# Key sums side by side, copied by two engines, and a choice whose second half moves: a linear-attention and mixture-of-experts kernel

## The chip, the cores and the metric

The kernel runs on one core of a Trainium2 chip. A core has TensorE (PE, matrix products; its weight loads are shown apart as PEld), VectorE (DVE), ScalarE (ACT), GpSimd (POOL) and SyncE (SP, which here starts DMA transfers). Each engine takes its own instructions in order and waits on semaphores for the others. PSUM is the memory that TensorE writes; it lies in banks of 512 float32 per partition. The metric is device time in microseconds (us).

## The reference

Linear attention over 8 batches, 8 heads, 576 tokens and 64 dimensions, with 128 random features, and then a layer of 8 experts to which each of the 4608 tokens is sent by its largest logit:

```python
q_p, k_p = phi(q_s), phi(k_s)              # exp of projections less their maximum
kv = np.einsum('bhsm,bhsd->bhmd', k_p, v)  # key sums
z = np.sum(k_p, axis=2)
num = np.einsum('bhsm,bhmd->bhsd', q_p, kv)
den = np.einsum('bhsm,bhm->bhs', q_p, z)[..., None] + 1e-06
x = (num / den) as [4608, 512]
logits = xn @ en.T / tau                   # xn, en: rows over their norms
expert_idx = np.argmax(logits, axis=1)
out[mask] = gate_w[mask, None] * (np.maximum(x[mask] @ w1[e], 0.0) @ w2[e])
```

## The kernel before, in words

The tokens are cut into 36 tiles of 128. Two batches share nine tiles, and so a key sum (over one batch) closes after the fourth-and-a-half and the ninth tile of a group: eight closes in all. One loop (L652 to L737) does attention; its iteration i handles keys of tile i and queries of tile i - 6, so iterations 0 to 5 have keys alone, 6 to 35 both, 36 to 41 queries alone (the tail), and 42 the last numerators. After the loop come a table of expert steps, worked out on VectorE while TensorE does filler work, and the expert part, 38 steps of matrix products.

Inside an iteration the order is written out by hand for all five engines. The names that the text uses, with what they do:

- `proj` (L321): projections, k in one PSUM bank and q in another; each iteration does two pairs, "one" and "two". Each pair is four products for two banks.
- `maxima` (L329), on VectorE: the largest of 128 features of four heads, `nmk` for keys and `nmq` for queries. `feats` (L334), on ScalarE: the exponentials.
- `qtr` (L395): transposes of the query features of the tile before into the two banks of `nub`; the prediction calls it the turn. `qcopy` (L403) copies one bank with ScalarE and the other with VectorE into `qp`.
- `num` (L412): query features times key sums, into the same two banks. `num_out` (L422), on VectorE: `rr` (denominator and its inverse), `xr` (the tile's rows), `lg` (their logits).
- `kvmm` (L341): key features times values, added up in two banks, `kv0` for one half of the heads and `kv1` for the other. The values have a column of ones, which gives z.
- `kv_closed` (L358): a finished key sum is copied to `kvs` by ScalarE in two halves, and by GpSimd into another order in `kvc`. In the next iteration `kv_turn` transposes it, `kv_turned` copies that back, `kv_logits` (kve in the prediction) multiplies it with the experts' vectors into the last columns of the second bank of `nub`, and `kv_logits_out` copies these into `kvs`.
- `routed` (L439): the choice for three tiles. Its steps: the logits' sum; their maximum `mx` and `raw`; the selection `sel` (L465 to L467, three steps on VectorE); the prefix, eight small products (L473, L475) into the second bank of `nub`; `base` and `run` (L481, L482) on VectorE, which read it; and then places and stores by GpSimd.
- `first_steps` (L542): expert work that is known early, taken out step by step with `next(fill)` as filler.

Work that is to be done at a place of a later iteration is put into tables by place: `mid`, `after`, `then` and `ends`, in the order in which the iteration comes to them (`mid` behind `qcopy`, `after` behind `num`, `then` ahead of `kvmm`, `ends` at its end). L730 says at which places the steps of a choice stand.

Of the kernel before, what the change touches and what calls it, by code (L numbers as in the profile page):

```python
# [11 lines left out]
F32 = mybir.dt.float32  # L12
# [4 lines left out]
AF = mybir.ActivationFunctionType  # L17
ALU = mybir.AluOpType
# [4 lines left out]
P = 128  # L23
B, H, S, D, M = 8, 8, 576, 64, 128
# [15 lines left out]
NPRE = 2  # L40
PADP = 6
FILLS = 1, 2, 2, 2, 2, 0
FILL1, FILL2, FILL3 = 6, 11, 6
# [12 lines left out]
def attention_moe(ctx: ExitStack, tc: tile.TileContext, qT, kT, v1, omT, emb, tau, w1q, w2q, xs, out):  # L56
# [222 lines left out]
    with ExitStack() as c1:  # L279
# [61 lines left out]
        def kvmm(i, a, b):  # L341
# [7 lines left out]
            for h in range(4):  # L349


                for c in range(0, P, 64):
# [3 lines left out]
                    )  # L356

        def kv_closed(sb, b):  # L358
            kvs[sb, b] = p1.tile([P, H, D + 1 + E], F32, name=f"kvs{sb}_{b}", tag="kvs", bufs=2)
            for a in range(2):  # L360
                nc.scalar.activation(kvs[sb, b][:, 4 * a : 4 * a + 4, 0 : D + 1], kva[sb, b, a], AF.Copy)
            kvc = xgp[NPRE][:, 0:DM].rearrange("p (h d) -> p h d", h=H)
            nc.gpsimd.tensor_copy(
                kvc.rearrange("p (c a) d -> p a c d", a=2), kvs[sb, b][:, :, 0:D].rearrange("p (a c) d -> p a c d", a=2)
            )
            st["kvc", sb, b] = kvc

        def kv_turn(sb, b):
            kvc = st["kvc", sb, b]
            st["kvtr", sb, b] = tr = ps.tile([P, 512], F32, name=f"kvtr{sb}_{b}", tag="kv0")  # L370
            for c in range(4):
                nc.tensor.transpose(tr[:, c * P : (c + 1) * P], kvc[:, 2 * c : 2 * c + 2, :].rearrange("p a d -> p (a d)"), ident)

# [15 lines left out]
        def kv_logits_out(sb, b):  # L389
            nc.vector.tensor_copy(  # L390
                kvs[sb, b][:, :, D + 1 :].rearrange("p (a c) e -> p c a e", a=2),
                st["kve", sb, b].rearrange("p c (a e) -> p c a e", a=2),
            )
# [15 lines left out]

        pn = nub[:, :, 0 : 4 * (D + 1 + E)].rearrange("p a (h w) -> p a h w", h=4)  # L410

        def num(i):  # L412
            sb, u = divmod(i, TPS)
            for a in range(2):
                for h in range(4):
                    for z, b in enumerate((u > 4, u >= 4)):
                        nc.tensor.matmul(
                            pn[z * 64 : z * 64 + 64, a, h, :], st["qp", i, z][:, 4 * a + h, :], kvs[sb, int(b)][:, 4 * a + h, :],
                            start=True, stop=True,
                        )  # L420

        def num_out(i):  # L422
# [3 lines left out]
            if gi == 0:  # L426
                st["lg", g] = small.tile([P, G, H, E], F32, name=f"lg{g}", tag="lg", bufs=2)
            rr = small.tile([P, 2, 4], F32, name=f"rr{i}", tag="rr", bufs=3)
            nc.vector.tensor_scalar(rr, pn[:, :, :, D], EPS, None, op0=ALU.add)
            nc.vector.reciprocal(rr, rr)  # L430
            by = lambda w: rr.unsqueeze(3).to_broadcast([P, 2, 4, w])
            nc.vector.tensor_tensor(
                xr[:, 0:DM].rearrange("p (h a d) -> p a h d", a=2, d=D), pn[:, :, :, 0:D], by(D), op=ALU.mult,
            )
            nc.vector.tensor_tensor(
                st["lg", g][:, gi].rearrange("p (a h) e -> p a h e", a=2), pn[:, :, :, D + 1 :], by(E), op=ALU.mult,
            )
# [200 lines left out]

        mid, after, then, ends = {}, {}, {}, {}
        at = lambda d, *key: d.setdefault(key, [])  # L640
# [4 lines left out]
        def go(d, *key):  # L645
            for f, *a in d.pop(key, ()):
                f(*a)
# [4 lines left out]
        for i in range(END + 1):  # L652
# [22 lines left out]
            elif qs:  # L675
                two = [("q", iq, a, ("px", "py")[i % 2]) for a in range(2)]
            proj(*one)
            if ts:
                qtr(iq - 1)
            for p in one[:1]:  # L680
                maxima(*p)
            proj(*two)
            if ts:
                qcopy(iq - 1, 1, True)
                qcopy(iq - 1, 0, False)
            go(mid, i)
            for p in one[:1]:
                feats(*p)
            if i == END:
                next(fill)  # L690
            for p in one[1:] or two[:1]:
                maxima(*p)
            if ts:
                num(iq - 1)
            go(after, i)
            for p in two[1:]:
                maxima(*p)
# [12 lines left out]
            for x in sums:  # L710
                kvmm(*x)
            closed = ss and u in (4, 8)
            if closed and not qs:
# [13 lines left out]
            if ts and iq % G == 0 and iq < NTILE:  # L727
                steps = routed(iq // G - 1)
                next(steps)
                for d, key in ((ends, i + 1), (mid, i + 2) if i >= NTILE else (ends, i + 1), (after, i + 2), (ends, i + 2), (ends, i + 2), (ends, i + 3), (ends, i + 4)):  # L730
                    at(d, min(key, END)).append((next, steps, None))
# [6 lines left out]
        loop.close()  # L738
        assert not any((mid, after, then, ends)), (mid, after, then, ends)
        steps = routed(NTILE // G - 1)  # L740
# [396 lines left out]
def layout(inputs):  # L1137
# [13 lines left out]
    for u in range(TPS + 1):  # L1151
        rows = slice(0, D) if u == 4 else slice(D, P) if u == 5 else slice(0, P)
        v1[:, u, rows, :, :D] = v[:, u - (u > 4), rows]
        v1[:, u, rows, :, D] = 1
    v1 = v1.reshape(NSB * (TPS + 1), P, H, D + 1)
# [28 lines left out]
```

## Time and profile before

| | |
|---|---|
| median of 3 runs | 657.77 us (657.25 to 657.97) |
| profiled execution | 658.2 us, span 656.4 us |
| PE busy | 631.7 us (96%) |
| DVE busy | 497.3 us (76%) |
| ACT busy | 416.9 us (64%) |
| POOL busy | 328.5 us (50%) |
| granted TensorE clock, mean | 0.996 of full speed |

A row of the profile names the line, the engine, the operation, the tile written and the tiles read, with partitions x elements. In a wait the engine on the left waited for the one on the right. A busy TensorE need not be one at its peak, since matrix products are pipelined and their ends are modelled. Attention with its tail lasts to about 217 us, and the expert part from there to the end.

### The profile page before, as it was taken

The numbers are of one execution on the slowest core, as the hardware profiler recorded it, in microseconds if no ns is written. First come the engines' busy times: TensorE is split into PE (matmuls) and PEld (weight loads), VectorE is DVE, ScalarE is ACT, GpSimd is POOL, SyncE is SP. The second block draws the span as 40 slices with busy tenths as digits, with TensorE's granted clock in tenths as the row PEclk, the third lists the DMA queues.
The fourth block names the chain that finished last, engine by engine and source line by source line (L and its number), as shares of the span: only waits on it lengthen the run. The fifth ranks groups of instructions, "written<-read, shape, count | busy, mean of one in ns | idle before, by whom it ended". The sixth has DMA issues, their size and how long they took to land. (4 is left out here: it accounts for less than half of the span.)

```text
span 656.4 us, 18641 instructions
## 1 busy us (share of the span) xinstructions
PE 631.7 (96%) x6339; PEld 532.1 (81%) x6340; DVE 497.3 (76%) x952; ACT 416.9 (64%) x1074; POOL 328.5 (50%) x414
## 2 busy tenths in 40 slices
PE   8999999998889999999999999999999999999993
PEld 7899999988877787888788888888888888888872
DVE  4789888899888736778787777777768787777771
ACT  6899899899877236645656565656555656565430
POOL 2013443448885425474556364646455554646352
PEclk9999999999999999999999999999999999999998
DMA  7547667678832388588898888978697878887710
GB/s 252 177 148 228 196 202 212 214 243 285 261 125 97 118 308 259 156 237 198 237 211 223 208 227 190 240 193 232 178 244 184 236 192 196 225 208 212 187 64 34
DMA packets 142362, 131.89 MB, mean 201 GB/s; under 512 B 106742, under 2 KB 106870, under 8 KB 142272
## 3 DMA queue, kind: packets, MB, share of 16 engines
q1 hardware_dynamic: 135808, 110.04, 62.8%
q0 software_dynamic: 6320, 20.38, 7.9%
q8 instruction: 57, 0.93, 0.6%
q10 hardware_dynamic: 144, 0.26, 0.2%
q14 instruction: 33, 0.27, 0.1%
HBM read 83.78 MB, written 21.97 MB: 161 GB/s over the span
## 5 line engine op out<-in xcount | busy, mean ns | idle before, releaser
L241 PE MATMUL nu<-w2h,hl 128*128 (+1 forms) x288 | 113.9, 395 | 0.4 <-DVE hl L948 0.4
L241 PE MATMUL nu<-w2h,hh 128*128 (+1 forms) x288 | 113.9, 396 | 0.0
L241 PE MATMUL nu<-w2l,hh 128*128 (+1 forms) x288 | 113.8, 395 | 0.0
L241 PE MATMUL pa<-w1h,xl 128*128 (+1 forms) x280 | 110.8, 396 | 0.4 <-DVE xl L947 0.4
L241 PE MATMUL pa<-w1h,xh 128*128 (+1 forms) x280 | 111.1, 397 | 0.0
L241 PE MATMUL pa<-w1l,xh 128*128 (+1 forms) x280 | 110.6, 395 | 0.0
L909 ACT ACTIVATE pl<-pa 128x512 uint16<-128x512 uint16 x68 | 40.1, 594 | 94.2 <-PE pa L241 56.0
L905 DVE TENSOR_REDUCE wd<-t 128x1024 uint16<-128x1024 uint16 x68 | 90.0, 1325 | 1.7 <-DMA t<-pl 1.7
L338 ACT ACTIVATE ftk<-pjk,nmk 128x128 f32<-128x128 f32 x288 | 84.9, 427 | 6.3 <-DVE nmk L331 6.0
L207 POOL TENSOR_TENSOR w1l<-raww,w1h 128x1024 f32 x34 | 83.7, 2461 | 7.4 <-DVE w1h L206 5.5
L905 DVE TENSOR_REDUCE pl<-pa 128x512 uint16<-128x512 uint16 x68 | 46.6, 688 | 51.6 <-ACT pl L909 51.5
L338 ACT ACTIVATE ftq<-pjq,nmq 128x128 f32<-128x128 f32 x288 | 80.0, 430 | 8.7 <-DVE nmq L331 7.8
L207 POOL TENSOR_TENSOR w2l<-raww,w2h 128x1024 f32 x34 | 82.1, 2415 | 2.4 <-issue 2.4
L327 PE MATMUL pjq<-om,qt 64*128 64x128 f32 x576 | 75.6, 283 | 1.1 <-ACT ftk L338 0.7
L327 PE MATMUL pjk<-om,kt 64*128 64x128 f32 x576 | 76.3, 285 | 0.3 <-DVE om L602 0.3
L944 ACT ACTIVATE hh<-wd 128x1024 fp32r<-128x1024 f32 x34 | 36.1, 1062 | 60.2 <-DVE wd L905 54.3
L327 PEld LDWEIGHTS pjk<-om,kt 64*128 64x128 f32 x576 | 65.1, 190 | 2.9 <-DVE om L602 0.6
L271 POOL DMA_INDIRECT y<-xgp x20 | 22.7, 1136 | 87.6 <-DVE xgp L248 84.1
L241 PEld LDWEIGHTS nu<-w2h,hl 128*128 128x128 f32 x288 | 54.0, 188 | 13.9 <-DVE hl L948 0.8
L327 PEld LDWEIGHTS pjq<-om,qt 64*128 64x128 f32 x576 | 63.9, 188 | 1.6 <-ACT ftk L338 0.9
L241 PEld LDWEIGHTS nu<-w2l,hh 128*128 128x128 f32 x288 | 54.1, 188 | 13.1
L241 PEld LDWEIGHTS nu<-w2h,hh 128*128 128x128 f32 x288 | 54.1, 188 | 13.0
(311 smaller groups left out, 1270.0 us busy)
## 6 DMA issues: line engine op xcount, KB each, us to landing
raww<-w1q SPq DMA_DIRECT2D x38, 512.0 KB, 3.9
raww<-w2q SPq DMA_DIRECT2D x38, 512.0 KB, 5.2
qt<-qT SPq DMA_DIRECT2D x36, 256.0 KB, 4.3
kt<-kT SPq DMA_DIRECT2D x35, 256.0 KB, 3.0
xgp<-xs SPq DMA_DIRECT2D x20, 260.5 KB, 2.8
xg<-xs SPq DMA_DIRECT2D x18, 260.5 KB, 2.9
rf<-w1q SPq DMA_DIRECT2D x4, 512.0 KB, 5.6
rf<-w2q SPq DMA_DIRECT2D x4, 512.0 KB
```

The source lines that it names most:

```text
L207: il = nc.gpsimd.tensor_tensor(at(l, dp), raw, at(h, dp).bitcast(F32), op=ALU.subtract)
L241: done.append(nc.tensor.matmul(dst, x[:, c * P : (c + 1) * P], ws.rearrange("p o f -> p (o f)"), start=(begin and i == 0 and k == 0), stop ...
L271: w = nc.gpsimd.indirect_dma_start(out=out, out_offset=bass.IndirectOffsetOnAxis(ap=xg[:, PAY - 1 : PAY].bitcast(I32), axis=0), in_=xg[:, ...
L327: nc.tensor.matmul(st["pj" + w, i, a][:, c, :], st[w, i][r, c, :], om[r, :], start=True, stop=True)
L338: nc.scalar.activation(ft[:, h, :], pj[:, h, :], AF.Exp, bias=nm[:, h : h + 1])
L905: nc.vector.tensor_reduce(to, src.unsqueeze(2), axis=AX.X, op=ALU.max)
L909: nc.scalar.activation(planes[1][:, o : o + 512], halved(src)[:, :, 1], AF.Copy)
L944: nc.scalar.activation(hh, wd[:, 0:F], AF.Relu)
```

## The change

Four things, in the diff's order.

Key sums: a head of the first half now has its logit columns and the ones ahead of its 64 values, a head of the second half has them behind, so that the values of two heads touch in `kvs`. ScalarE copies one half and VectorE the other. The transposes read `kvs`, and GpSimd's copy goes. The first bank of `nub` gets `num` from column 132 on, the second from column 0, so that one access pattern (`heads`) reaches both.

Query-only iterations (36 to 41): the query projections stand ahead of `qtr`, the first maximum ahead of `qcopy`, the second behind it.

Filler: in iterations 39 to 41 one step is taken between `qcopy` and `num`, and one less at the end.

The choice of the main loop (nine of them, in iterations 11, 14, ... 35): the selection moves from the end of the iteration before to the place `then`, and the prefix from `after` to a new place `late`, behind `kvmm`.

```diff
@@ -39,7 +39,7 @@
 LAG = 6
 NPRE = 2
 PADP = 6
-FILLS = 1, 2, 2, 2, 2, 0
+FILLS = 1, 2, 1, 1, 1, 0
 FILL1, FILL2, FILL3 = 6, 11, 6
 NSTAT = 38
 WARM = 26
@@ -355,21 +355,20 @@
                         start=begin and h == 0, stop=u == 4 + 4 * b and h == 3,
                     )
 
+        HW = D + 1 + E
+
+        def spread(x, *dims):
+            return bass.AP(tensor=x.tensor, offset=x.offset, ap=[x.ap[0], *([a, n] for a, n in dims)])
+
         def kv_closed(sb, b):
-            kvs[sb, b] = p1.tile([P, H, D + 1 + E], F32, name=f"kvs{sb}_{b}", tag="kvs", bufs=2)
-            for a in range(2):
-                nc.scalar.activation(kvs[sb, b][:, 4 * a : 4 * a + 4, 0 : D + 1], kva[sb, b, a], AF.Copy)
-            kvc = xgp[NPRE][:, 0:DM].rearrange("p (h d) -> p h d", h=H)
-            nc.gpsimd.tensor_copy(
-                kvc.rearrange("p (c a) d -> p a c d", a=2), kvs[sb, b][:, :, 0:D].rearrange("p (a c) d -> p a c d", a=2)
-            )
-            st["kvc", sb, b] = kvc
+            kvs[sb, b] = p1.tile([P, 4, 2 * HW], F32, name=f"kvs{sb}_{b}", tag="kvs", bufs=2)
+            nc.scalar.activation(kvs[sb, b][:, :, E : HW], kva[sb, b, 0], AF.Copy)
+            nc.vector.tensor_copy(kvs[sb, b][:, :, HW : HW + D + 1], kva[sb, b, 1])
 
         def kv_turn(sb, b):
-            kvc = st["kvc", sb, b]
             st["kvtr", sb, b] = tr = ps.tile([P, 512], F32, name=f"kvtr{sb}_{b}", tag="kv0")
             for c in range(4):
-                nc.tensor.transpose(tr[:, c * P : (c + 1) * P], kvc[:, 2 * c : 2 * c + 2, :].rearrange("p a d -> p (a d)"), ident)
+                nc.tensor.transpose(tr[:, c * P : (c + 1) * P], kvs[sb, b][:, c, E + 1 : E + 1 + P], ident)
 
         def kv_turned(sb, b):
             kvt = xgp[NPRE][:, 0:DM].rearrange("p (c m) -> p c m", c=4)
@@ -388,7 +387,7 @@
 
         def kv_logits_out(sb, b):
             nc.vector.tensor_copy(
-                kvs[sb, b][:, :, D + 1 :].rearrange("p (a c) e -> p c a e", a=2),
+                spread(kvs[sb, b].rearrange("p c w -> p (c w)"), (2 * HW, 4), (HW + D + 1, 2), (1, E)),
                 st["kve", sb, b].rearrange("p c (a e) -> p c a e", a=2),
             )
 
@@ -407,7 +406,14 @@
                 tc.declare_no_dep(c.ins, st["cp", 1].ins.name, reason="another bank")
 
 
-        pn = nub[:, :, 0 : 4 * (D + 1 + E)].rearrange("p a (h w) -> p a h w", h=4)
+        flat = nub.rearrange("p a x -> p (a x)")
+        o0 = P + E // 2
+        pn = [nub[:, a, o : o + 4 * HW].rearrange("p (h w) -> p h w", h=4) for a, o in ((0, o0), (1, 0))]
+
+        def heads(o, at1, n):
+
+            x = 512 + at1 - o0 - o
+            return flat[:, o0 + o : o0 + o + 2 * x].rearrange("p (a x) -> p a x", a=2)[:, :, 0 : 4 * HW].rearrange("p a (h w) -> p a h w", h=4)[:, :, :, 0:n]
 
         def num(i):
             sb, u = divmod(i, TPS)
@@ -415,7 +421,7 @@
                 for h in range(4):
                     for z, b in enumerate((u > 4, u >= 4)):
                         nc.tensor.matmul(
-                            pn[z * 64 : z * 64 + 64, a, h, :], st["qp", i, z][:, 4 * a + h, :], kvs[sb, int(b)][:, 4 * a + h, :],
+                            pn[a][z * 64 : z * 64 + 64, h, :], st["qp", i, z][:, 4 * a + h, :], kvs[sb, int(b)][:, h, a * HW : (a + 1) * HW],
                             start=True, stop=True,
                         )
 
@@ -426,14 +432,14 @@
             if gi == 0:
                 st["lg", g] = small.tile([P, G, H, E], F32, name=f"lg{g}", tag="lg", bufs=2)
             rr = small.tile([P, 2, 4], F32, name=f"rr{i}", tag="rr", bufs=3)
-            nc.vector.tensor_scalar(rr, pn[:, :, :, D], EPS, None, op0=ALU.add)
+            nc.vector.tensor_scalar(rr.unsqueeze(3), heads(E, D, 1), EPS, None, op0=ALU.add)
             nc.vector.reciprocal(rr, rr)
             by = lambda w: rr.unsqueeze(3).to_broadcast([P, 2, 4, w])
             nc.vector.tensor_tensor(
-                xr[:, 0:DM].rearrange("p (h a d) -> p a h d", a=2, d=D), pn[:, :, :, 0:D], by(D), op=ALU.mult,
+                xr[:, 0:DM].rearrange("p (h a d) -> p a h d", a=2, d=D), heads(E + 1, 0, D), by(D), op=ALU.mult,
             )
             nc.vector.tensor_tensor(
-                st["lg", g][:, gi].rearrange("p (a h) e -> p a h e", a=2), pn[:, :, :, D + 1 :], by(E), op=ALU.mult,
+                st["lg", g][:, gi].rearrange("p (a h) e -> p a h e", a=2), heads(0, D + 1, E), by(E), op=ALU.mult,
             )
 
         def routed(g):
@@ -636,7 +642,7 @@
             nc.vector.tensor_copy(enbd[D:P, :, 1, :], ev[D:P])
 
 
-        mid, after, then, ends = {}, {}, {}, {}
+        mid, after, then, late, ends = {}, {}, {}, {}, {}
         at = lambda d, *key: d.setdefault(key, [])
         for i, f in ((1, emb0), (2, emb1), (4, emb2), (5, emb3)):
             at(ends, i).append((f,))
@@ -674,26 +680,31 @@
                 one = [("k", i, a, ("px", "py")[i % 2]) for a in range(2)]
             elif qs:
                 two = [("q", iq, a, ("px", "py")[i % 2]) for a in range(2)]
-            proj(*one)
+            proj(*(one if ks else two))
             if ts:
                 qtr(iq - 1)
-            for p in one[:1]:
+            for p in (one if ks else two)[:1]:
                 maxima(*p)
-            proj(*two)
+            if ks:
+                proj(*two)
             if ts:
                 qcopy(iq - 1, 1, True)
                 qcopy(iq - 1, 0, False)
+            for p in () if ks else two[1:]:
+                maxima(*p)
             go(mid, i)
+            if NTILE + 2 < i < END:
+                next(fill)
             for p in one[:1]:
                 feats(*p)
             if i == END:
                 next(fill)
-            for p in one[1:] or two[:1]:
+            for p in one[1:]:
                 maxima(*p)
             if ts:
                 num(iq - 1)
             go(after, i)
-            for p in two[1:]:
+            for p in two[1:] if ks else ():
                 maxima(*p)
             u = (i - 1) % TPS
             sums = [(j, a, b) for j, b in ([(i - 2, 1)] if u == 5 else []) + [(i - 1, int(u > 4))] for a in range(2)] if ss else []
@@ -709,6 +720,7 @@
                     maxima(*p)
             for x in sums:
                 kvmm(*x)
+            go(late, i)
             closed = ss and u in (4, 8)
             if closed and not qs:
                 kv_closed((i - 1) // TPS, u // 4 - 1)
@@ -727,7 +739,7 @@
             if ts and iq % G == 0 and iq < NTILE:
                 steps = routed(iq // G - 1)
                 next(steps)
-                for d, key in ((ends, i + 1), (mid, i + 2) if i >= NTILE else (ends, i + 1), (after, i + 2), (ends, i + 2), (ends, i + 2), (ends, i + 3), (ends, i + 4)):
+                for d, key in ((ends, i + 1), (mid if i >= NTILE else then, i + 2), (after if i >= NTILE else late, i + 2), (ends, i + 2), (ends, i + 2), (ends, i + 3), (ends, i + 4)):
                     at(d, min(key, END)).append((next, steps, None))
             go(ends, i)
             if NTILE < i <= END:
...
@@ -1150,8 +1162,10 @@
     v1 = np.zeros((NSB, TPS + 1, P, H, D + 1), v.dtype)
     for u in range(TPS + 1):
         rows = slice(0, D) if u == 4 else slice(D, P) if u == 5 else slice(0, P)
-        v1[:, u, rows, :, :D] = v[:, u - (u > 4), rows]
-        v1[:, u, rows, :, D] = 1
+        v1[:, u, rows, 0::2, 1:] = v[:, u - (u > 4), rows, 0::2]
+        v1[:, u, rows, 0::2, 0] = 1
+        v1[:, u, rows, 1::2, :D] = v[:, u - (u > 4), rows, 1::2]
+        v1[:, u, rows, 1::2, D] = 1
     v1 = v1.reshape(NSB * (TPS + 1), P, H, D + 1)
     w2 = np.asarray(inputs["moe_w2"]).reshape(E, NQ, 2, P, DM).transpose(0, 1, 3, 2, 4)
     return {
```

TensorE around the choice of iteration 11, before. `sel` is the selection, `tri` and `one` are constants, `kva` the key sum of `kvmm`, `pjk` and `pjq` the next iteration's projections; `num` stands above these rows.

```order
L475 LDWEIGHTS one_75
L475 MATMUL nub<-sel_127,one_75 64x16
L475 LDWEIGHTS one_75
L475 MATMUL nub<-sel_127,one_75 64x8
L353 MATMUL kva_0_0_1014<-vt10v,ftk_0_1045 64x65 x8
L353 MATMUL kva_0_1_1023<-vt10v,ftk_1_973 64x65 x8
L327 MATMUL pjk_1_1202<-om,kt_920 128x128
L327 MATMUL pjq_0_1203<-om,qt_924 128x128
```

And in the changed kernel, from the last product of `num` on (`kvs`, `qp`); the rest of the prefix and then the projections follow.

```order
L423 MATMUL nub<-kvs_1_911,qp_1_1101 64x73
L353 MATMUL kva_0_0_1012<-vt10v,ftk_0_1043 64x65 x8
L353 MATMUL kva_0_1_1021<-vt10v,ftk_1_971 64x65 x8
L479 LDWEIGHTS tri
L479 MATMUL nub<-sel_127,tri 64x32
L481 LDWEIGHTS one_75
L481 MATMUL nub<-sel_127,one_75 64x24
L481 LDWEIGHTS one_75
L481 MATMUL nub<-sel_127,one_75 64x16
```

The prefix has moved behind the 16 instructions of `kvmm`.

VectorE at the same place, before: maximum and difference of the logits, the selection, and the first rows of iteration 11 up to `rr`.

```order
L460 TENSOR_TENSOR raw0_916<-raw0_916,mx0_1051 128x24
L465 SCALAR_TENSOR_TENSOR sel0_127<-raw0_916,iotm_83 128x24
L466 TENSOR_REDUCE mx0_1051<-sel0_127 128x3
L467 TENSOR_TENSOR sel0_127<-iotm_83,mx0_1051 128x24
L331 TENSOR_REDUCE nmk11_1_1094<-pjk11_1_1068 128x4
L405 COPY qp4_0_1108<-nub_126 128x512
L331 TENSOR_REDUCE nmq5_0_1115<-pjq5_0_1069 128x4
L331 TENSOR_REDUCE nmq5_1_1141<-pjq5_1_1097 128x4
L331 TENSOR_REDUCE nmk11_0_1148<-pjk11_0_1096 128x4
L429 TENSOR_SCALAR rr4_1168<-nub_126 128x8
```

And in the changed kernel.

```order
L466 TENSOR_TENSOR raw0_914<-raw0_914,mx0_1049 128x24
L331 TENSOR_REDUCE nmk11_1_1089<-pjk11_1_1063 128x4
L404 COPY qp4_0_1103<-nub_126 128x512
L331 TENSOR_REDUCE nmq5_0_1110<-pjq5_0_1064 128x4
L331 TENSOR_REDUCE nmq5_1_1128<-pjq5_1_1092 128x4
L471 SCALAR_TENSOR_TENSOR sel0_127<-raw0_914,iotm_83 128x24
L472 TENSOR_REDUCE mx0_1049<-sel0_127 128x3
L473 TENSOR_TENSOR sel0_127<-iotm_83,mx0_1049 128x24
L331 TENSOR_REDUCE nmk11_0_1138<-pjk11_0_1091 128x4
L435 TENSOR_SCALAR rr4_1166<-nub_126 128x8
```

The three rows of the selection have moved from ahead of four full passes (`nmk`, `qp`, `nmq`, `nmq`) to behind them; `rr` follows one pass later.

VectorE in the tail, iteration 38, before: from a split of early expert work (`w1h`) to the first read of `num`.

```order
L229 TENSOR_TENSOR w1h_106<-fs_x0_4699,w1h_106 128x512
L405 COPY qp31_0_4737<-nub_126 128x512
L465 SCALAR_TENSOR_TENSOR sel1_128<-raw9_4585,iotm_83 128x24
L466 TENSOR_REDUCE mx9_4690<-sel1_128 128x3
L467 TENSOR_TENSOR sel1_128<-iotm_83,mx9_4690 128x24
L331 TENSOR_REDUCE nmq32_0_4742<-pjq32_0_4725 128x4
L331 TENSOR_REDUCE nmq32_1_4768<-pjq32_1_4726 128x4
L429 TENSOR_SCALAR rr31_4772<-nub_126 128x8
```

And in the changed kernel.

```order
L229 TENSOR_TENSOR w1h_106<-fs_x0_4691,w1h_106 128x512
L331 TENSOR_REDUCE nmq32_0_4727<-pjq32_0_4701 128x4
L404 COPY qp31_0_4731<-nub_126 128x512
L331 TENSOR_REDUCE nmq32_1_4733<-pjq32_1_4702 128x4
L471 SCALAR_TENSOR_TENSOR sel1_128<-raw9_4577,iotm_83 128x24
L472 TENSOR_REDUCE mx9_4682<-sel1_128 128x3
L473 TENSOR_TENSOR sel1_128<-iotm_83,mx9_4682 128x24
L435 TENSOR_SCALAR rr31_4764<-nub_126 128x8
```

One maximum now stands ahead of the copy `qp`, the other one and the selection behind it.

## Rows read from the trace of the kernel before

**Rows 1.** Stages of the run: length, busy time by engine, clock, DMA, GB/s.

```profile
41.00:172.00 131.00, 127.14 (x2958) 120.38 (x2956) 117.55 (x298) 120.67 (x424) 62.07 (x169) 1.00 0.70 220
...
217.00:600.00 383.00, 381.88 (x1670) 306.66 (x1669) 285.09 (x457) 214.45 (x398) 200.73 (x110) 1.00 0.82 215
```

**Rows 2.** Waits of TensorE over the run: us in total, times, longest.

```profile
PE nub L417 <- DVE qp L405: 5.1, 8, 1.7
PE nub L400 <- DVE run L482: 1.8, 3, 0.9
...
PE nub L400 <- DVE lg L435: 0.6, 1, 0.6
```

**Rows 3.** Order of time, TensorE, one iteration without a choice: start, length, instruction.

```profile
51.83 0.66 PE L400 MATMUL nub<-ident,ftq 64*128 64x64 f32 x16
...
53.48 1.25 PE L417 MATMUL nub<-kvs,qp 128*64 128x73 f32 x32
...
55.59 0.37 PE L327 MATMUL pjk<-om,kt 64*128 64x128 f32 x1
...
56.58 0.66 PE L400 MATMUL nub<-ident,ftq 64*128 64x64 f32 x16
```

**Rows 4.** Order of time, TensorE and VectorE, one iteration with a choice.

```profile
46.62 0.18 DVE L465 SCALAR_TENSOR_TENSOR sel<-raw,iotm 128x24 bf16<-128x24 f32 x1
...
46.67 0.66 PE L400 MATMUL nub<-ident,ftq 64*128 64x64 f32 x16
...
47.15 0.68 DVE L331 TENSOR_REDUCE nmk<-pjk 128x4 f32<-128x512 f32 x1
...
48.58 1.25 PE L417 MATMUL nub<-kvs,qp 128*64 128x73 f32 x32 [0.30 <-DVE qp L405]
...
49.62 0.18 PE L473 MATMUL nub<-sel,tri 128*64 128x32 bf16 x1
...
49.75 0.17 PE L475 MATMUL nub<-sel,one 128*64 128x8 bf16 x1
...
50.14 0.16 DVE L429 TENSOR_SCALAR rr<-nub 128x8 f32<-128x8 f32 x1
...
51.51 0.16 DVE L482 TENSOR_TENSOR run<-run,nub 128x8 f32<-128x8 f32 x1
```

**Rows 5.** Order of time, an iteration with a key-sum turn and no choice.

```profile
167.55 1.25 PE L417 MATMUL nub<-kvs,qp 128*64 128x73 f32 x32
...
168.67 0.65 PE L384 MATMUL nub<-enbd,xgp 128*64 128x16 f32 x16
...
169.44 0.17 DVE L429 TENSOR_SCALAR rr<-nub 128x8 f32<-128x8 f32 x1 [0.22 <-PE nub L384]
```

**Rows 6.** Order of time, a choice in the query-only tail.

```profile
211.49 0.27 PE L475 MATMUL nub<-sel,one 128*64 128x24 bf16 x6
...
213.56 0.71 PE L400 MATMUL nub<-ident,ftq 64*128 64x64 f32 x16 [0.21 <-DVE run L482]
```

**Rows 7.** Order of time, last choice of the loop and the tail.

```profile
177.19 0.66 PE L400 MATMUL nub<-ident,ftq 64*128 64x64 f32 x16
177.47 0.65 DVE L465 SCALAR_TENSOR_TENSOR sel<-raw,iotm 128x24 bf16<-128x24 f32 x1
...
183.74 0.72 PE L400 MATMUL nub<-ident,ftq 64*128 64x64 f32 x16 [0.92 <-DVE run L482]
...
185.74 1.25 PE L417 MATMUL nub<-kvs,qp 128*64 128x73 f32 x32 [0.33 <-ACT qp L405]
...
191.08 1.25 PE L417 MATMUL nub<-kvs,qp 128*64 128x73 f32 x32
...
195.81 1.25 PE L417 MATMUL nub<-kvs,qp 128*64 128x73 f32 x32 [0.30 <-DVE qp L405]
```

**Rows 8.** Instructions by line and shape: count, busy us, mean ns, idle before.

```profile
L405 DVE COPY qp<-nub 128x512 f32<-128x512 f32 x36 | 24.6, 683 | 3.0 <-PE nub L400 3.0
...
L361 ACT ACTIVATE kvs<-kva 128x260 f32<-128x260 f32 x16 | 6.1, 488 | 0.0
```

More of the change, by code (lines that the diff above doesn't have):

```diff
@@ L738, in attention_moe @@
         loop.close()
-        assert not any((mid, after, then, ends)), (mid, after, then, ends)
+        assert not any((mid, after, then, late, ends)), (mid, after, then, late, ends)
         steps = routed(NTILE // G - 1)
```

## The prediction

> **What bounds the kernel now.** I read the stages first, then TensorE's waits, then the order of time inside single iterations. The stage table [rows 1] says that after 217 us TensorE is busy for 381.88 of 383 us: the expert part is bound by TensorE and has no hole, so what the attention part gains or loses reaches the end one to one. In the attention loop (41 to 172 us) TensorE is busy 127.14 of 131 us, VectorE 117.55, ScalarE 120.67: three engines near their limit, and half a microsecond moved on one shows on another. TensorE's waits in attention [rows 2] are few: 5.1 us before `num` for VectorE's copy `qp`, and 1.8 and 0.6 us before the query transposes (`qtr`, which I call the turn) for VectorE's reads of the banks that the turn overwrites.
>
> An iteration without a choice takes 4.75 us from turn to turn (51.83 to 56.58): `num` follows the turn after 1.65 us, and the next key projections follow `num` after 2.11 us (53.48 to 55.59) [rows 3]. In one with a choice [rows 4] the selection stands ahead of the maxima on VectorE (46.62 to 47.15), `num` comes late (48.58, 1.91 us behind the turn), the prefix matmuls follow `num` at 49.62 with `kvmm` behind them, and VectorE reads `num` from 50.14 on. Its last read of the bank, the `run` update, ends at 51.67; the next turn stands at 51.83 [rows 3]. That turn has no slack against `run` already.
>
> **The change, part by part.**
>
> The second half of the choice. Nine iterations of the main loop get the selection behind the query maxima and the prefix behind `kvmm`. The gain is plain: `qp` no longer stands behind the selection, and `num` comes at 1.65 us again, as in [rows 3]. The price stands on VectorE. Its first read of `num`, `rr`, waits for more than `num`. [Rows 5] show it in an iteration without a choice: `num` ended at 168.80, the kve matmuls behind it, which write other columns of the second bank, at 169.32 (168.67 + 0.65), and `rr` began at 169.44, 0.12 us after kve, with 0.22 us of waiting put down to it. In the built program `rr` waits in the choice iterations for the last prefix matmul, before the change and after it; only that matmul now stands behind 16 `kvmm` instructions instead of directly behind `num`.
>
> The Trainium skill (PSUM — Partial Sum Buffer, section PSUM bank collisions raise a hardware error) has the rule for it: guard PSUM by bank and quadrant with semaphores, not by address. The 0.12 us behind kve agree with it [rows 5]. By that rule the sum is the one below; guarded by address alone, `rr` would start behind `num`, and the sum would be that of the second rival.
>
> The period from turn to turn is then: 1.65 to `num` and 2.11 to the end of what `kvmm` issues [rows 3], 0.30 for the prefix (49.62 to 49.75 + 0.17 [rows 4]), and from the prefix's end over `rr` and `run` to the turn 1.80, as [rows 6] show it once (211.49 + 0.27 = 211.76 to 213.56, with 0.21 us of TensorE waiting for `run` although filler work stood between): 5.86 us. The projections between prefix and turn cover about 1 of the 1.80 us; TensorE idles for the other 0.8. VectorE by itself would allow 5.4 (0.2 from turn to first maximum, five passes 47.15 to 50.14, selection 0.53, 1.69 from `rr` to the turn [rows 4]), so the prefix decides.
>
> Before, the nine periods were 5.16 (first, 46.67 to 51.83), 5.16, 5.31, 5.16, 5.00, 5.31, 5.17, 6.27 and 6.55 (last, 177.19 to 183.74) [rows 3, 4, 7]. In the second, fifth and eighth a key sum closes in the same iteration, and the new VectorE copy stands between the last `num` read and the `run` read. Its length is not in the trace: VectorE takes 0.16 for 8 elements (`rr` [rows 4]) and 0.68 for 512, ScalarE 0.49 for this very shape [rows 8]. I take 0.35, as it has half of the 512 elements on the same engine; the ends are 0.16 and 0.68. In the last two iterations the selection is slow (one step 0.65 [rows 7], 1.0 in all) beside GpSimd work, and leaves that much; a weight cast stays ahead of the maxima, so `num` comes at 2.0 and 2.3 us. The differences are 0.70, 1.05, 0.55, 0.70, 1.21, 0.55, 0.69, 0.31 and -0.02: +5.7 us.
>
> What comes back. With TensorE held once in three iterations, ScalarE and VectorE catch up, and ScalarE has one copy of 0.49 less per close [rows 8], so waits elsewhere shrink. At most the whole idle time of TensorE in the loop comes back, 131 - 127.14 = 3.9 us [rows 1]; the larger part of it is `num`'s wait in the choice iterations, which the periods above count already. Ends 0 and -3.9; I take -1.2, the part that is not that wait.
>
> Key sums. GpSimd's eight copies go; they lay beside projections, so I count nothing for them. Eight VectorE copies come. In the closes without a choice they lie between the last `num` read and the end of the next projections and are hidden there; without that cover they cost 0.35 each, 1.8 for five, which the range holds.
>
> The query-only tail. Projections ahead of the turn cover its waits for VectorE, 2.4 us at most [rows 2]. But the first query maximum (0.60 a pass) then stands ahead of the `qp` copy on VectorE, and nothing stands between turn and `num` on TensorE where no filler is put. In the first iteration `num` comes 1.6 behind the turn (turn 0.72 [rows 7], copy 0.68 [rows 8], two hand-overs of 0.1) for 2.00 (183.74 to 185.74 [rows 7]): -0.4. In the third, 191.08 to 195.81 [rows 7], VectorE's chain sets the time (reads of `num`, choice, split, copy), and the maximum is added to it: +0.6. The other iterations trade a wait before the turn for one before `num` of much the same size; I take -0.1 for them. That is +0.1; ends -2.4 (the waits go and nothing comes) and +3.6 (0.60 in each of six). The filler steps taken in the loop are ten before and after, so none moves out of it.
>
> The sum is +5.7 - 1.2 + 0.1 = +4.6 us on the profiled execution's 658.2 (span 656.4 and 1.8 around it): 662.8. The median of the runs is 657.77, 0.4 below it: **662.4 us**.
>
> **Rivals.**
>
> First, the waits go and none takes their place: `num`'s 5.1 us and the turns' 2.4 [rows 2] are 7.5 at most, so 650 at the best, 653 with half of it. For it: the selection does stand in front of `qp` now. Against it: the turn behind [rows 4] has no slack against `run`, whatever becomes of `num`. 0.13.
>
> Second, no difference: the hold is given back in full (+5.7 - 3.9 - 2.4 is -0.6), or VectorE does not wait for the late prefix, and the choice costs VectorE's 5.4 where 5.45 was the mean. Both end near 657.8. For it: three engines are close, and slack on one is used by another. Against it: the 0.12 us of [rows 5]. 0.14.
>
> Third, slower than forecast: nothing comes back and VectorE becomes the bound of the tail, +5.7 + 3.6: 667. It decides once the copies of the closes also delay the maxima behind them. Against it: VectorE's 117.55 of 131 us in the loop leave it some idle time [rows 1]. 0.10.
>
> **How the numbers follow.** The forecast has 0.63, with a range of its own of 660 to 665 from what comes back and the tail. Taking in the no-difference case, with 1.2 us below it as its own spread, and most of the third gives 656.6 to 666.0. About 0.2% (1.3 us) is what measurements of this kernel can tell from no change: slower 0.63 + 0.10 = 0.73, same 0.14, faster 0.13.
>
> **What would show it.** Right: in nine iterations TensorE waits 0.6 to 1.2 us before the turn with VectorE's `run` update as releaser, `rr` starts about 0.12 us after the last prefix matmul, `num` no longer waits for `qp` in the first seven, and the periods are near 5.9 (6.2 where a close falls in). VectorE's key-sum copy takes 0.3 to 0.5. In the tail there is almost no wait before turns, and 0.3 to 1 before `num` where no filler stands. Wrong: if `rr` starts while `kvmm` runs, the step on the bank falls; if the periods are 5.9 and the end is not later, what comes back was taken too small.

## The result

The changed kernel takes 661.20 us (median of 8 runs, 659.42 to 662.97) where the kernel before takes 657.76 (8 runs, 657.25 to 658.96): a ratio of 1.0053, with a 95% interval of 1.0038 to 1.0068, so 3.5 us slower (2.5 to 4.5). In a second set of runs (below) the ratio was 1.0055 (1.0038 to 1.0071). The forecast was 662.4, slower.

The profiled execution of the changed kernel has a span of 659.6 us. The waits of TensorE in it answer to [rows 2]: engine and line that waited, what was waited for, us in total, times, longest.

```profile
PE nub L399 <- DVE run L488: 6.8, 10, 1.0
PE nub L423 <- DVE qp L404: 2.5, 6, 0.9
PE nub L423 <- ACT ftq L338: 2.3, 2, 1.4
```

The wait of `num` for the copy `qp` has halved, and the wait of the turn for the `run` update has grown from 1.8 to 6.8 us: nine in the main loop and one in the tail. The order of time of TensorE and VectorE in iteration 11, the first with a choice, shows where it comes from (it answers to [rows 4]):

```profile
46.63 0.66 PE L399 MATMUL nub<-ident,ftq 64*128 64x64 f32 x16
46.83 0.69 DVE L331 TENSOR_REDUCE nmk<-pjk 128x4 f32<-128x512 f32 x1 [0.28 <-PE pjk L327]
...
48.26 1.24 PE L423 MATMUL nub<-kvs,qp 128*64 128x73 f32 x32
...
49.23 0.17 DVE L471 SCALAR_TENSOR_TENSOR sel<-raw,iotm 128x24 bf16<-128x24 f32 x1
49.30 1.13 PE L353 MATMUL kva<-vt10v,ftk 128*64 128x65 f32 x32
...
49.75 0.68 DVE L331 TENSOR_REDUCE nmk<-pjk 128x4 f32<-128x512 f32 x1
50.23 0.18 PE L479 MATMUL nub<-sel,tri 128*64 128x32 bf16 x1
...
50.29 0.24 PE L481 MATMUL nub<-sel,one 128*64 128x16 bf16 x5
...
50.64 0.17 DVE L435 TENSOR_SCALAR rr<-nub 128x8 f32<-128x8 f32 x1 [0.21 <-PE nub L481]
...
52.02 0.16 DVE L488 TENSOR_TENSOR run<-run,nub 128x8 f32<-128x8 f32 x1
...
52.24 0.53 PE L399 MATMUL nub<-ident,ftq 64*128 64x64 f32 x10 [0.62 <-DVE run L488]
```

`num` comes 1.63 us behind the turn, no longer 1.91. But the prefix, which was at 49.62 in front of `kvmm`, is now at 50.23 behind it; its last product ends at 50.53, and `rr` starts 0.11 us later, though `num` was done at 49.50. The trace names the prefix as what `rr` waited for. VectorE runs on without a pause from there to `run`, and the turn waits for that. The period is 52.24 - 46.63 = 5.61 us, for 5.16 before. The rows show a second thing: VectorE stands idle for 0.28 us ahead of the first maximum, in the place where the selection used to be [rows 4].

Periods from turn to turn, each the difference of two turn starts, in iterations 11, 14, ... 35 (those where a key sum closes are marked *):

```
iteration   11    14*   17    20    23*   26    29    32*   35    sum
before     5.16  5.16  5.30  5.16  5.00  5.31  5.17  6.27  6.55  49.08
changed    5.61  5.95  5.85  5.61  6.06  5.84  6.28  6.49  6.79  54.48
```

The nine are 5.4 us longer; the other periods from iteration 7 to 35 are 1.1 us shorter in sum (107.49 for 108.56), and the six of the tail 0.6 longer (30.38 for 29.82). The turn of iteration 42 stands at 218.60 for 213.56: 5.0 us later, 0.15 of it from ahead of iteration 7.

### The profile page after: what moved, and what is told of

Its sections match the earlier page's. It is cut to its first block, busy times and chain, and to the rows that moved or that the text cites. A ratio compares the mean times of both kernels' runs of the same rounds, so it can differ in the third digit from the quotient of the medians.

```text
span 659.6 us, 18622 instructions
## 1 busy us (share of the span) xinstructions
PE 631.6 (96%) x6339; PEld 533.1 (81%) x6340; DVE 499.4 (76%) x960; ACT 415.0 (63%) x1066; POOL 322.2 (49%) x406
```

## The experiments

Each ran beside runs of the kernel before on the same chip, and a ratio, with its 95% interval, is to those; it need not be the quotient of the two medians shown. Iteration, turn and choice are as above.

**The choice back at its old places.** In the line that places the steps:

```diff
-(ends, i + 1), (mid if i >= NTILE else then, i + 2), (after if i >= NTILE else late, i + 2),
+(ends, i + 1), (mid, i + 2) if i >= NTILE else (ends, i + 1), (after, i + 2),
```

> The changed kernel with the choice of the main loop back at its old places (selection at the end of the iteration before, prefix right behind num); key sums, query-only tail and fillers stay changed. Theory (the moved choice is what costs): the nine choice iterations fall back from 5.6 to 6.8 us to about 5.2 (6.3 and 6.5 for the last two), 5.4 us in all, some 1 us of waits elsewhere returns, and the time is 657 to 658.3, no difference from the kernel before. Rival (VectorE's key-sum copies or the tail cost): the time stays at 660 or above though the choice iterations are short.

Measured: 663.54 us for 663.35 of the kernel before, 0.999 (0.9973 to 1.0007). Times on this chip are higher for every kernel, and the changed kernel itself was not run on it. With the choice at its old places no loss is left, so the key sums and the tail by themselves don't make one. The undisturbed choice periods are 5.15, 5.35 and 5.35 us (iterations 11, 17, 26). In iterations 16, 19, 22 and 25 all four kernels profiled on this chip show periods 0.2 to 0.9 us longer than in the two first profiles, with idle time of TensorE that the profile partly puts down to "issue". I did not find their cause; from here on I compare single periods where nothing of that kind stands.

**The move alone, in the kernel before.** The same line the other way in the kernel before, with `go(late, i)` added behind `kvmm`.

> The kernel before with the move of the main loop's choice alone (selection to the place then, prefix behind kvmm); key sums, tail and fillers as before. Theory: the same loss as the whole change, 660.5 to 662.5, with periods of about 5.6 us in the first choice iterations. Rival (the loss needs VectorE's key-sum copies): 658 to 659.

Measured: 665.27 for 663.35, 1.0025 (1.0011 to 1.0039), so +1.7 us: slower, as the theory has it, but by less than it said, and the period of iteration 11 is 5.62 as in the changed kernel. So there is a loss without VectorE's key-sum copies. Its size is another matter: in the three choice iterations with a close the periods are 5.60, 5.60 and 5.90 us, for 5.95, 6.06 and 6.49 of the changed kernel, so some 1.4 us of the loss may have come with the copies. The comparison is between chips, and the unexplained waits lie in the same stretch; how much the move costs without the new key sums stays open.

**Selection at the old place, prefix at the new one.**

```diff
-(ends, i + 1), (mid if i >= NTILE else then, i + 2), (after if i >= NTILE else late, i + 2),
+(ends, i + 1), (mid, i + 2) if i >= NTILE else (ends, i + 1), (after if i >= NTILE else late, i + 2),
```

> The changed kernel with the selection at its old place and the prefix at its new one, behind kvmm. Theory (rr waits for the last prefix matmul, so the prefix's place decides): num comes 1.9 us behind the turn, the prefix 1.97 behind num, 0.26 long, rr 0.13 behind it and the next turn 1.6 behind rr: periods of 5.9 us, 0.25 above those of the changed kernel, time 662 to 664. Rival (VectorE's row of passes decides and the wait for the prefix is by the way): with the selection in the hole ahead of the first maximum the periods are 5.2 to 5.3 and the time is 657.5 to 659.

Measured: 670.83 for 663.35, 1.0104 (1.0082 to 1.0126): 7 us above the kernel before, more than expected. The period of iteration 11 is 52.50 - 46.62 = 5.88, where 5.9 stood. The same places of the order of time:

```profile
46.62 0.66 PE L399 MATMUL nub<-ident,ftq 64*128 64x64 f32 x16
...
48.52 1.24 PE L423 MATMUL nub<-kvs,qp 128*64 128x73 f32 x32 [0.30 <-DVE qp L404]
49.49 0.68 DVE L331 TENSOR_REDUCE nmk<-pjk 128x4 f32<-128x512 f32 x1
...
50.55 0.24 PE L481 MATMUL nub<-sel,one 128*64 128x16 bf16 x5
50.90 0.17 DVE L435 TENSOR_SCALAR rr<-nub 128x8 f32<-128x8 f32 x1 [0.73 <-PE nub L481]
```

VectorE was through with its maxima at 50.17 and stood for 0.73 us, until 0.11 us behind the last prefix product. Waits of VectorE for the prefix, from 41 to 200 us, are here

```profile
DVE rr L435 <- PE nub L481: 6.9, 9, 1.0
```

all nine of them, and in the changed kernel

```profile
DVE rr L435 <- PE nub L481: 1.4, 5, 0.5
```

That settles what `rr` waits for: the last prefix product, though `num` was done at 49.76 (48.52 + 1.24).

**Prefix ahead of kvmm.** In the changed kernel, the prefix at `after` in place of `late`. A choice takes its steps in order, and `after` comes ahead of `then`; so the selection in fact ran at `after`, one maximum earlier, and the prefix at `then`, in front of `kvmm`.

```diff
-(mid if i >= NTILE else then, i + 2), (after if i >= NTILE else late, i + 2),
+(mid if i >= NTILE else then, i + 2), (after, i + 2),
```

> The changed kernel with the prefix back right behind num, the selection at its new place between the maxima. If the prefix's place alone costs: rr finds the prefix done, periods of 5.2, time 657 to 658.5. If the selection's place costs too (it left a hole of 0.3 us on VectorE ahead of the first maximum and now lengthens the unbroken row of passes up to rr): rr starts right behind the last maximum, periods of 5.4, TensorE waits about 0.4 us for the selection ahead of the prefix, time 659 to 660.5. If the wait for the selection pushes kvmm and the projections onto the path as well: as the changed kernel, 661 or more.

Measured: 663.98 for 663.35, 1.0013 (0.9994 to 1.0031). The time can't tell the first two expectations apart; it rules out the third. The period does: 5.31 us in iterations 11, 17, 20 and 26. VectorE does not wait at `rr` any more:

```profile
49.23 0.18 PE L479 MATMUL nub<-sel,tri 128*64 128x32 bf16 x1
...
49.68 0.68 DVE L331 TENSOR_REDUCE nmk<-pjk 128x4 f32<-128x512 f32 x1
50.28 0.15 DVE L435 TENSOR_SCALAR rr<-nub 128x8 f32<-128x8 f32 x1
...
51.65 0.16 DVE L488 TENSOR_TENSOR run<-run,nub 128x8 f32<-128x8 f32 x1
...
51.87 0.71 PE L399 MATMUL nub<-ident,ftq 64*128 64x64 f32 x16 [0.26 <-DVE run L488]
```

It works on in one row up to `run`, with the selection inside. The four arrangements in the undisturbed iteration 11 are then: both steps at the old places 5.15, selection moved and prefix early 5.31, both new 5.61 (5.62 on this chip, in the kernel before), selection old and prefix late 5.88. The late prefix costs 0.73 us with the old selection and 0.30 with the moved one; the selection's move costs 0.16 with an early prefix and gives back 0.27 with a late one. In the 5.31 the selection stands one maximum earlier than in the changed kernel, so these differences hold to the extent that this maximum does not matter.

**The whole change and its other parts on one chip.** The changed kernel again, unaltered:

> The changed kernel once more, unaltered, so that it stands on the same chip as the parts of the change. Theory (period of a choice iteration up by 0.45 us where nothing else waits, loss in the loop about 4 to 5 us, some given back): 2.5 to 4.5 us slower than the kernel before on that chip. Rival (the loss was an accident of single runs): within 1.3 us of it.

Measured: 661.12 for 657.07, 1.0055 (1.0038 to 1.0071). The nine choice periods add up to 53.93 us (54.48 in the first profile), and all but those of iterations 14, 23 and 35 agree with it within 0.02.

The tail and the fillers as before, the rest changed (the lines of the loop that stand under `if ks` put back, `FILLS = 1, 2, 2, 2, 2, 0`):

> The changed kernel with the query-only iterations and the fillers as before; key sums and the choice stay changed. If the tail's change costs the 0.56 us that the turns of the two first profiles differ by (4.48 us behind at the turn of iteration 36, 5.04 at that of 42): 0.5 us faster than the changed kernel beside it. Rival (the new tail saves waits, and the 0.56 us is the choice's echo): 0.5 to 2 us slower than the changed kernel.

Measured: 661.01, again 1.0055 (1.0038 to 1.0071). In the trace the six tail periods are 29.22 us for 30.38 of the changed kernel beside it; in the time the two are equal, and the intervals (1.1 us to either side) are too wide to say whether the 1.2 us of the trace are given back behind the tail; they leave room for 0.5 us either way, so the two expectations can't be told apart.

The key sums alone (the diff's second to sixth piece and its last one, on the kernel before):

> The kernel before with the new key-sum layout and its two copies alone; choice, tail and fillers as before. If VectorE's copies are hidden and GpSimd's copies no longer hold the transposes: key-sum turns 0.05 to 0.2 us shorter in each of eight, time 0 to 1.5 us below the kernel before. Rival (VectorE pays 0.42 us for each of eight copies): 1.5 to 3.4 us above it.

Measured: 656.15 for 657.07, 0.9984 (0.9971 to 0.9996): 1.0 us faster (0.3 to 1.9). Groups of instructions of the transposes, before and with the new key sums: count, busy us, mean ns, and idle time ahead of them with its releaser.

```profile
L372 PEld LDWEIGHTS kvtr<-ident,xgp 128*128 128x128 f32 x32 | 3.4, 140 | 2.1 <-POOL xgp L363 2.0
```

```profile
L371 PEld LDWEIGHTS kvtr<-ident,kvs 128*128 128x128 f32 x32 | 3.4, 140 | 1.0
```

The weight loads of the transposes waited 2.0 us in all for GpSimd's copy; the products of the transposes stood for 0.3 us of that. Now they wait for no copy. The periods of iterations 10, 15, 19 and 24, which have such transposes, go from 6.10, 6.91, 6.13 and 7.00 to 5.96, 6.77, 5.98 and 6.76 us; 28 and 33 are longer (6.47 for 6.10, 7.12 for 6.97), and over the six 0.15 us is left. So the trace agrees with a gain at the transposes but does not show that the 1.0 us comes from there.

**One VectorE instruction less at the end of the choice.** On the key sums alone, `base` and `run` in one:

```diff
...
-base = new("base", [P, G, E])
-nc.vector.tensor_tensor(base, pr[:, 0:G], run.unsqueeze(1).to_broadcast([P, G, E]), op=ALU.add)
-nc.vector.tensor_tensor(run, run, pr[:, G], op=ALU.add)
+both = new("base", [P, G + 1, E])
+base = both[:, 0:G]
+nc.vector.tensor_tensor(both, pr, st.get("run", run).unsqueeze(1).to_broadcast([P, G + 1, E]), op=ALU.add)
+st["run"] = both[:, G]
...
```

Left out is that the last choice copies the sum back to `run`, and that the table reads `st["run"]`.

> The kernel before with the new key sums, and with base and run worked out by one VectorE instruction over all four blocks of the prefix instead of two. In a choice iteration the next turn waits for the second of the two. Theory (what stands on VectorE between the last prefix matmul and the turn is on the path): some 0.15 to 0.2 us less in each of the choice iterations, 1 to 2 us below the kernel with the layout alone. Rival (TensorE's projections cover the end of the choice where the prefix stands early): within 0.5 us of it.

Measured: 655.81, 0.9979 (0.9966 to 0.9993), against 0.9984 without it: no difference that can be told. The period of iteration 11 is 5.15 with it and without it, and those of 14, 17, 20 and 26 agree within 0.03 us; iterations 23, 35, 38 and 41 are shorter by 0.18 or 0.19 us (29 is 0.33 shorter, 32 is 0.21 longer). For the five choices without a gain the rival holds: with an early prefix it is not `run` that ends the iteration.

**The choice's first step earlier.** Those rows left one wait in a choice iteration, that of `num` for `qp`, which stands behind the selection. On top of the last kernel:

```diff
-((ends, i + 1), (mid, i + 2) if i >= NTILE else (ends, i + 1),
+((ends if i >= NTILE else then, i + 1), (mid, i + 2) if i >= NTILE else (ends, i + 1),
```

> New key sums and the merged base and run, and the choice's first step (mx, raw: 0.36 us on VectorE) moved from the end of iteration i + 1 to the place then of it, ahead of rr. The selection so ends 0.3 us earlier, ahead of the time when the first maximum finds its projections. Theory (num waits in the choice iterations only because the selection delays the copy qp): num comes 1.65 instead of 1.91 us behind the turn, seven periods of 4.9 instead of 5.15, 1 to 2 us below the merged kernel: 0.9945 to 0.997 of the kernel before. Rival (0.36 us more ahead of rr pushes the turn of the choice iteration back by as much): 0.998 or more.

Measured: 653.30 us for 657.93, 0.9924 (0.9901 to 0.9948): 5.0 us below the kernel before (3.4 to 6.5), and by the ratios 0.55% below the merged kernel, which ran on another chip; more than expected, and faster than the kernel before and the changed one. Iterations 10 and 11, VectorE and TensorE:

```profile
44.00 0.17 DVE L465 TENSOR_REDUCE mx<-raw 128x3 f32<-128x24 f32 x1
...
46.71 0.18 DVE L473 TENSOR_TENSOR sel<-iotm,mx 128x24 bf16<-128x24 f32 x1
46.76 0.66 PE L399 MATMUL nub<-ident,ftq 64*128 64x64 f32 x16
46.96 0.69 DVE L331 TENSOR_REDUCE nmk<-pjk 128x4 f32<-128x512 f32 x1
...
48.40 1.24 PE L423 MATMUL nub<-kvs,qp 128*64 128x73 f32 x32
```

The selection ends at 46.89, before the first maximum would start anyhow, and `num` follows the turn after 1.64 us without a wait. The periods are 4.88 (iterations 11 and 20) and 5.06 (17 and 26), for 5.15, 5.24 and twice 5.36 of the merged kernel. The nine add up to 46.34 us, for 48.84. In these two profiles other iterations give 2.2 us of it back (13: 5.78 for 4.92; 31: 5.85 for 5.22), and the turn of iteration 42 comes no earlier (211.23, 211.12). So the rows show what the step does to its own iterations; the way from there to the medians they don't show, and single profiles differ by as much (below).

**The kernel before, a second profile.**

> The kernel before once more, unaltered, for a second profile. In the first two profiles the turn of iteration 42 lies 5.0 us later in the changed kernel, its span only 3.2; thirty products of the expert part take 7.00 us in the profile of the kernel before and 6.98 in both profiles of the changed one. If that pace belongs to the kernel, this profile shows 7.00 again; if it is drawn anew in each execution, it may show 6.98, and the expert part then is about 1.4 us shorter. The time is that of the kernel before.

Measured: 657.41 for 657.93, 0.9995 (0.9978 to 1.0012). Products of the expert part at the same place, the kernel before in the first profile and in the second, 30 products apart:

```profile
399.73 0.39 PE L241 MATMUL pa<-w1l,xh 128*128 x1
...
406.73 0.39 PE L241 MATMUL nu<-w2l,hh 128*128 x1
```

```profile
399.73 0.40 PE L241 MATMUL pa<-w1h,xh 128*128 x1
...
406.71 0.40 PE L241 MATMUL nu<-w2h,hh 128*128 x1
```

7.00 us there, 6.98 here. Over a longer stretch the difference is firmer: the products that start at 409.76 and 589.89 us in the first profile are 772 apart, those at 409.72 and 589.82 in the second 775, so the second is 0.4% faster. So the pace does not belong to the kernel. In this profile the turn of iteration 42 stands at 212.94 and the span is 654.3.

Set against the second profile of the changed kernel, which was taken on another chip, this one gives 49.66 us for the nine choice periods (53.93 in the changed kernel), 107.63 for the other periods up to iteration 35 (107.52), 29.75 for the tail (30.38), and the turn of iteration 42 stands 5.1 us earlier (212.94, 218.07). The loss in the choice iterations (4.3 us) and in the tail (0.6) is there again; the 1.1 us that the other periods gave back in the first two profiles is not.

## Why the prediction was right

- **What bounds it.** What attention loses reaches the end, in the main: 5.0 us at the turn of iteration 42, 3.2 at the end of the span (659.6 for 656.4), and the pace of the expert part accounts for most of what lies between (under the total, below). The same two stages of the changed kernel as in [rows 1]:

```profile
41.00:172.00 131.00, 123.42 (x2846) 115.57 (x2844) 116.41 (x296) 114.38 (x406) 55.21 (x158) 1.00 0.68 214
217.00:600.00 383.00, 381.03 (x1710) 308.02 (x1710) 284.64 (x461) 214.51 (x398) 202.22 (x118) 1.00 0.81 213
```

  TensorE is idle for 2 us of the expert part, 1.1 before, so there is next to nothing in it that could take a loss up. In the same stretch of the loop all engines have more idle time than before: TensorE waits more and the others wait with it.
- **`rr` waits for the last prefix product.** Right. It starts 0.11 us behind it, in the changed kernel and with the old selection, where the wait is 0.73 us long. The Trainium skill (PSUM — Partial Sum Buffer, section PSUM bank collisions raise a hardware error) would have PSUM guarded by bank and quadrant, not by address. The trace agrees: where the prefix is late, `rr` starts behind products that write other columns of a bank it reads. Where the prefix is early (5.31 us), `rr` finds it done and nothing is lost to it. The wait is part of the built program; no run left it out, so what would happen without it is not shown.
- **The period of 5.86 us.** The mechanism is right, the size 0.25 too large in iteration 11: 1.63 to `num` (1.65 forecast), 1.97 from there to the prefix (2.11), 0.30 for the prefix (0.30), 1.71 from its end to the turn (1.80), 5.61 in all. The 2.11 was the time to the next projections; the prefix starts sooner behind `kvmm`. The wait before the turn is 0.62 or 0.63 us in the five choices without a close up to iteration 29, as forecast, and 0.18, 0.96 and 0.96 in the three with one. The sum over nine came out near, 5.4 for 5.7 (4.3 in the second profiles), and in part by luck, with errors of both signs: four of the first six were taken 0.15 to 0.26 too long, iterations 29 and 35 (6.28 and 6.79, forecast 5.86 and 6.53) too short.
- **"So the prefix decides."** Half of it. With the prefix early and the selection moved the period is 5.31, not 5.15: the selection left a hole of VectorE ahead of the first maximum for a place inside its unbroken row of passes. I had put that row at 5.4 without drawing the conclusion that the move would cost something even with an early prefix.
- **The key-sum copy on VectorE.** 0.42 us (forecast 0.35, between 0.16 and 0.68), and the first two choice iterations with a close are 0.34 and 0.45 us longer than that of iteration 11. The group in the changed kernel:

```profile
L366 DVE COPY kvs<-kva 128x260 f32<-128x260 f32 x8 | 3.4, 419 | 0.0
```

- **What comes back, -1.2 us.** Not shown, neither size nor reason. The other periods are 1.1 us shorter in the first two profiles and 0.1 in the second ones, so that the agreement of the first pair is luck as far as one can tell. I counted nothing for GpSimd's copies and laid the gain to engines that catch up; the key sums alone are 1.0 us faster (0.3 to 1.9), so "I count nothing for them" put at nothing a part that is not nothing. That the gain comes from transposes that no longer wait for GpSimd's copy fits the trace and is not shown by it.
- **The tail, +0.1.** +0.6 in both pairs of profiles, nothing that the times can tell. Two of its terms can be read in the order of time, changed kernel:

```profile
188.22 0.71 PE L399 MATMUL nub<-ident,ftq 64*128 64x64 f32 x16 [0.66 <-DVE run L488]
189.81 1.24 PE L423 MATMUL nub<-kvs,qp 128*64 128x73 f32 x32 [0.88 <-DVE qp L404]
...
195.08 1.24 PE L423 MATMUL nub<-kvs,qp 128*64 128x73 f32 x32 [0.94 <-ACT ftq L338]
...
198.98 0.68 DVE L331 TENSOR_REDUCE nmq<-pjq 128x4 f32<-128x512 f32 x1
...
199.58 0.68 DVE L404 COPY qp<-nub 128x512 f32<-128x512 f32 x1
...
200.40 1.24 PE L423 MATMUL nub<-kvs,qp 128*64 128x73 f32 x32 [1.40 <-ACT ftq L338]
```

  `num` came 1.59 us behind the first turn, as forecast, but the period fell by 0.10 only (4.68 for 4.78): the projections that stood between the two now stand behind `num`, ahead of the next turn, and I had counted only their leaving. From `num` to `num` of the third iteration 5.32 us pass, for 4.73 before [rows 7]: the +0.6 of the forecast. The row lays the wait to ScalarE's `ftq`, but `num` starts 0.14 us behind the end of VectorE's copy `qp` (199.58 + 0.68), which stands behind the first maximum, as forecast. Of the signs named for the tail, the turns of iterations 37 to 41 don't wait, but that of 42 waits 0.91 us for `run`; `num` waits 0.88, 0.94 and 1.40 us in the first three iterations, for 0.3 to 1.
- **The total.** +4.6 forecast, +3.5 measured, and 5.0 in the traces at the turn of iteration 42. From there to the span's end it takes 1.8 us less than in the kernel before (441.0 for 442.8). The products of the expert part run 0.4% apart in two profiles of one kernel, and 0.4% of some 430 us, by my estimate about 1.7 us, is thus the chance of single executions; the two first profiles lie on either side of it. The parts measured on one chip are -0.16% for the key sums, +0.71% for the choice on top of them (1.0055 / 0.9984) and nothing for the tail: -1.0 + 4.6 + 0 = 3.6 us. They add up to the whole by construction, as each run is set against the next, so the sum proves nothing; the one other measure of the move, in the kernel before and on another chip, is +1.7 us.

The rival of vanishing waits failed as it was argued: half of `num`'s wait went, and the turn's came. The rival of no difference failed at the 0.11 us. The third, 667, failed at the tail, which cost 0.6 in the traces for its 3.6; whether anything came back in the loop, its other term, is open.

## What to carry to other kernels

Where a small product shares a PSUM bank with results that VectorE is about to read, its place on TensorE can set when that read starts, as it did here by 0.73 us; so try it in front of long work. Before a step is moved on an engine, look whether its old place was a hole. Here the hole was 0.28 us, the selection 0.53, and its move into the unbroken row cost 0.16 us of the period even with an early prefix. The wait that a change takes away shows what is next only when that iteration's other chain is added up too; here the better way to remove it was to bring the selection's input forward by one place (653.30 us, with the new key sums and the merged instruction).

## What the runs showed of the hardware

The products of the expert part run at one of two paces: thirty take 7.00 us, or 6.96 to 6.98. From 410 to 590 us the pace is fixed within each of the twelve profiles, five at the slower one and seven at the faster; the kernel before showed both, and the granted clock of that stretch is 1.00 both times. What sets it is open. By the estimate above it makes single profiles of a kernel of this length differ by some 1.7 us behind the same instruction, so that a loss of a few us is read from the periods of the stage and from medians, not from two spans.
